# Fifteen short TensorE products and one pair of scores moved in the opening of a fused attention and feed-forward kernel

## The chip, the cores and the metric

The kernel runs on one core of a Trainium2 chip. The metric is the device time of one execution in microseconds (us); less is better. Engines are named as in the profile: PE is TensorE's matmul, PEld its weight load, DVE is VectorE, ACT is ScalarE, POOL is GpSimd, SP is SyncE.

## What is computed

Softmax attention for 8 batches and 12 heads (448 positions, head width 64), then a feed-forward layer with a leaky ReLU on the 3584 x 768 result:

```python
scores = (1 / sqrt(64)) * q @ k.transpose(0, 1, 3, 2)
attn = softmax(scores, axis=-1)
x = (attn @ v).transpose(0, 2, 1, 3).reshape(3584, 768)
h = x @ w_in                       # 768 -> 2048
out = maximum(0.01 * h, h) @ w_out # 2048 -> 768
```

## The kernel before

**Units.** The attention is cut into 48 units of two heads of one batch. Six units (HP) make up one batch's rows. A unit goes through the same steps: load q, k, v by DMA; cast them to bf16 (`cast`, L183; L190 for q and k, L198 for v); turn q and k with eight TensorE transposes and one copy out of PSUM (`transposes`, L294; products at L301, copy at L305); four pairs of score products (`scores`, L311, products at L319, one pair for each quarter of 112 keys); four exponentials on ScalarE (`expo`, L326; the first three write tile `e` at L331, the fourth writes tile `c` at L334); two weighted sums, one for each head (`pv`, L366, sixteen small products at L362 in `pairs`), each followed on VectorE by a reciprocal (L374) and a product (L375) into tile `x`; last, four transposes of `x` (`x_transposes`, L379, L389 and copy at L390).

**Order.** The instruction order of each engine is written out by hand in program order. `first(u)` (L870) issues the first six units as a software pipeline: the scores and exponentials of unit u, the transposes of unit u + 1, the weighted sums of unit u - 1, the x transposes of unit u - 2. After these six, the feed-forward products fill TensorE, and a hand-made model decides where the attention steps of later batches go among them.

**PSUM.** Two banks `g0` and `g1` rotate through `next_bank()` (L74); they hold the transposes and the weighted sums. Three slots `sc0` to `sc2`, of two banks each, rotate through `next_slot()` (L69) and hold the scores; a slot is free when the exponential that reads it has ended. `next_bank()` reverses the list and returns `banks[1]`, so `banks[0]` is the one handed out before the latest.

**Products on zeros.** `warm_up` (L239) issues 128x512 products and `stay_warm` (L243) 128x128 products on a tile of zeros (`warm`, part of `h_mix`, so `hmix` in the profile). Their results are never read. In the kernel before, seven long ones come at the start, one and five short ones behind the two halves of unit 0's transposes (L303), and one long one between unit 0's third and fourth scores (L878).

**What happens in the first units.** In `first(0)` unit 1's transposes follow unit 0's fourth scores on TensorE, then come the casts of unit 2 and of unit 0's v on VectorE (L894, L895). In `first(1)` three scores of unit 1 are followed by unit 2's transposes, unit 0's first weighted sum (`pv(0, 0)`), unit 1's fourth scores (L899) and, at the end, unit 0's second weighted sum (`pv(0, 1)`).

Of the kernel before, what the change touches and what calls it, by code (L numbers as in the profile page):

```python
# [16 lines left out]
def kernel(  # L17
# [9 lines left out]
    nc = tc.nc  # L27
# [3 lines left out]
    P = 128  # L31
# [34 lines left out]
    banks = [ps_g.tile([P, 4 * P], F32, name=f"g{i}") for i in range(2)]  # L66
    slots = [ps_s.tile([P, 2, 512], F32, name=f"sc{i}") for i in range(3)]

    def next_slot():  # L69

        slots.append(slots.pop(0))
        return slots[-1]

    def next_bank():  # L74

        banks.reverse()
        return banks[1]
# [105 lines left out]
    def cast(u, parts=(0, 1, 2), by=nc.gpsimd.tensor_copy):  # L183
        if u >= NU:
            return
        for x in parts:
            f = raw[u].pop(x)
            t = qkb[u % NB]
            if x < 2 and (x == 0 or u < HY):
                by(t[:SC, x].rearrange("p so h d -> p h so d"), f)  # L190
            elif x == 1:
                if u < HY + NB:
                    nc.gpsimd.memset(t[:, 1, KC], 0.0)
                by(t[:, 1, :KC].rearrange("p so h d -> p h so d"), f[:, :, :KC])
                by(t[:D, 1, KC, 0], f[:D, 0, KC])
                by(t[D:, 1, KC, 1], f[:D, 1, KC])
            elif u < HY:
                by(v_old[:, u % NV, :, :, :D], f)  # L198
            else:
                t = v_sb[u % NV]  # L200
                by(t[:, :2 * KC, :D].rearrange("p (h so) d -> p h so d", h=2), f[:, :, :KC])  # L201
                by(t[:D, 2 * KC, :D], f[:D, 0, KC])
                by(t[D:, 2 * KC + 1, :D], f[:D, 1, KC])
# [27 lines left out]
    warm = h_mix.rearrange("p m c t -> p (m c t)")[:, :512]  # L231
# [7 lines left out]
    def warm_up(n):  # L239
        for _ in range(n):  # L240
            nc.tensor.matmul(next_bank(), warm[:, :P], warm, start=True, stop=True)

    def stay_warm(n):  # L243

        ps = next_slot()
        for _ in range(n):
            nc.tensor.matmul(ps[:, 0, :P], warm[:, :P], warm[:, :P], start=True, stop=True)

    warm_up(7)
    nc.vector.memset(qkT_all.rearrange("p u i c s -> p u (i c s)")[:, :, 2 * S:2 * S + EP], 0.0)  # L250
# [39 lines left out]
    def turn_tile(bank):  # L290
        bank = next_bank() if bank is None else bank
        return bank.bitcast(BF16)

    def transposes(u, bank=None):  # L294
        n = SC if u < HY else P
        t, flat = qkb[u % NB], qkT[u % NQ].rearrange("p i c s -> p (i c s)")[:, :2 * NSC * n]
        for parts in ((1,), (0,)) if u == 0 else ((0, 1),):
            tr = turn_tile(bank)[:, :2 * NSC * n].rearrange("p (i s) -> p i s", i=2)
            for i in parts:
                for so in range(NSC):  # L300
                    nc.tensor.transpose(tr[:, i, ts(so, n)], t[:n, i, so].rearrange("p h d -> p (h d)"), ident[:n, :n])  # L301
            if u == 0:
                stay_warm(1 if parts == (1,) else 5)  # L303
            at = slice(parts[0], parts[-1] + 1)
            (nc.scalar.copy if u == 0 and parts == (1,) else nc.vector.tensor_copy)(  # L305
                flat.rearrange("p (i s) -> p i s", i=2)[:, at], tr[:, at]
            )
# [3 lines left out]
    def scores(u, c):  # L311
        ps = next_slot()
        t = qkT[u % NQ]
        sc_t[u, c] = ps
        if u < HY:
            t = t.rearrange("p i c s -> p (i c s)")
            for j in range(2):
                p = slice(j * D, (j + 1) * D)
                nc.tensor.matmul(ps[:, j, :S], t[p, S + c * SC:S + c * SC + P], t[p, :S], start=True, stop=True)  # L319
            return  # L320
        for p, j in ((slice(0, D), 0), (slice(D, P), 1)) if c < KC else ((slice(0, P), 0),):
            nc.tensor.matmul(  # L322
                ps[:, j, :S].rearrange("p (so s) -> p so s", so=NSC), t[p, 1, c], t[p, 0, :, :SC], start=True, stop=True,
            )

    def expo(u, c):  # L326
        e, ps = e_sb[u % NE], sc_t.pop((u, c))
        n = SC if u < HY else P
        if c < KC:
            e = e[:n, :EM].rearrange("p (j c s) -> p j c s", j=2, c=KC)  # L330
            nc.scalar.activation(e[:, :, c, :], ps[:n, :, :S], AX.Exp, scale=scale)  # L331
        elif u < HY:
            e = e_old[u % NE][:n, :2 * S].rearrange("p (j s) -> p j s", j=2)
            nc.scalar.activation(e, ps[:n, :, :S], AX.Exp, scale=scale)  # L334
        else:
            nc.scalar.activation(e[:, EM:EL], ps[:, 0, :S], AX.Exp, scale=scale)
# [29 lines left out]
    def pv(u, j, bank=None):  # L366

        bank = next_bank() if bank is None else bank
        ps = bank[:, :NSC * (D + 1)].rearrange("p (q d) -> p q d", q=NSC)
        pairs(u, j, ps)  # L370
        if j == 0:
            x_t[u] = x_pool.tile([SC, NSC, 2, D], BF16, name="x")
        rec = r_pool.tile([SC, NSC, 1], F32, name="rec")
        nc.vector.reciprocal(rec, ps[:SC, :, D:])  # L374
        nc.vector.tensor_mul(  # L375
            x_t[u][:, :, j, :], ps[:SC, :, :D], rec.to_broadcast([SC, NSC, D])
        )

    def x_transposes(u, bank=None):  # L379
        b, hp = divmod(u, HP)  # L380
        at = place_of(b * S)
        if bank is None:
            x = x_t.pop(u).rearrange("p so h d -> p so (h d)")
            turn(xT_flat[:, hp * NX + at:hp * NX + at + S], x.rearrange("p so n -> p (so n)"))
            return
        dst = xT[:, hp, at:at + S]
        tr = turn_tile(bank)
        for so in range(NSC):
            nc.tensor.transpose(tr[:, ts(so, SC)], x_t[u][:, so], ident[:SC, :SC])  # L389
        nc.vector.tensor_copy(dst, tr[:, :S])  # L390
# [467 lines left out]
    def supply(u):  # L858

        for what, n, *parts in {0: [('load', 6, (0, 1)), ('qk', 3), ('v', 1), ('v', 2), ('load', 6, (2,))], 1: [('qk', 4), ('v', 3), ('load', 8, (0, 1))], 2: [('qk', 5), ('v', 4), ('w', 1)], 3: [('qk', 6), ('v', 5), ('w', 1)], 4: [('qk', 7), ('v', 6), ('load', 10, (0, 1)), ('load', 8, (2,))], 5: [('qk', 8), ('v', 7), ('load', 10, (2,)), ('load', 12)]}[u]:  # L860
            if what == "qk":
                cast(n, (0, 1))
            elif what == "v":
                cast(n, (2,))
            elif what == "load":
                load(n, *parts)
            else:
                load_w(n)

    def first(u):  # L870

        scores(u, 0)
        scores(u, 1)
        if u < 2:
            scores(u, 2)
        expo(u, 0)
        if u == 0:
            warm_up(1)  # L878
        expo(u, 1)
        if u >= 2:  # L880
            x_transposes(u - 2, next_bank())
        if u == 1:
            transposes(u + 1)
        if u >= 1:
            pv(u - 1, 0)
        if u > 1:
            scores(u, 2)
            scores(u, 3)
        if u == 0:
            scores(u, 3)  # L890
        if u != 1:
            transposes(u + 1)
        if u == 0:
            cast(2, (0, 1), fast)  # L894
            cast(0, (2,), fast)  # L895
        if u + 1 < HP:
            supply(u)
        if u == 1:
            scores(u, 3)  # L899
        expo(u, 2)  # L900
        expo(u, 3)
        if u + 1 == HP:
            supply(u)
        if u >= 1:
            pv(u - 1, 1)
# [4 lines left out]
    for u in range(HP):  # L910
        first(u)
# [343 lines left out]
```

## Time and profile before

| | |
|---|---|
| median of 3 runs | 376.85 us |
| the three runs | 376.82, 376.85, 377.42 us |
| profiled execution: its own time | 376.9 us |
| profiled execution: span | 375.1 us |
| PE busy | 368.5 us (98% of the span) |
| DVE, ACT, POOL busy | 255.4, 259.9, 191.8 us |
| granted TensorE clock | 1.00 in the mean |

A line of the timeline has the start in us, the length in us, the engine, the line of the kernel, the operation, the tiles written and read, and the count of merged instructions. In square brackets stands the engine's idle time before it and what ended that. A line of the groups has the busy time in us and the mean of one in ns, then the idle time before such instructions. A line of the chain is one piece of the work that ended last: start, length, and what it was. Matmuls overlap: two or more merged in one line take less than the sum of their lengths, and the end of a matmul is modelled.

### The profile page before, as it was taken

The page shows a single profiled execution, that of the slowest core. Times are in us where ns is not written, and L with a number is a line of the kernel's source. Part 1 is how long each engine was busy: PE and PEld are TensorE (multiplying, and loading weights), DVE is VectorE, ACT ScalarE, POOL GpSimd, SP SyncE. Part 2 cuts the span into 40 slices and gives each one's busy share as a digit, 9 for nine tenths or more (in the row PEclk, how much of TensorE's full clock was granted, in tenths as well). Part 3 has the DMA queues.
Part 4 walks back from the last instruction along what each step waited for, and adds up shares of the span by engine and source line. Part 5 has one row for each costly group of instructions (what it writes and reads, how often), then busy time and mean ns, then how long its engine had stood idle before and what let it go on. Part 6 is the DMA issues. An engine that isn't in the chain of part 4 may idle for free.

```text
span 375.1 us, 10120 instructions
## 1 busy us (share of the span) xinstructions
PE 368.5 (98%) x4004; PEld 265.4 (71%) x4004; DVE 255.4 (68%) x560; ACT 259.9 (69%) x399; POOL 191.8 (51%) x376
## 2 busy tenths in 40 slices
PE   7899999999999999999999999999999999999996
PEld 3665658755698566995569966699665995679865
DVE  4664798767666967676576665875747775685864
ACT  6998795866768785758766587666787658626721
POOL 8976781987269979634488335692347020000000
PEclk9999999999999999999999999999999999999999
DMA  9999999999499967973979648989447640221123
GB/s 156 198 203 206 184 195 203 161 163 177 94 189 151 125 136 92 197 160 52 140 145 147 141 66 75 170 134 192 62 67 103 136 112 0 75 62 40 47 66 105
DMA packets 99920, 48.08 MB, mean 128 GB/s; under 512 B 64672, under 2 KB 96928, under 8 KB 99872
## 3 DMA queue, kind: packets, MB, share of 16 engines
q0 software_dynamic: 39600, 22.47, 45.4%
q1 hardware_dynamic: 60080, 24.84, 34.0%
q8 instruction: 31, 0.51, 0.6%
q14 instruction: 17, 0.14, 0.1%
q10 hardware_dynamic: 192, 0.12, 0.1%
HBM read 45.61 MB, written 11.01 MB: 151 GB/s over the span
## 4 chain that ended last, share of the span: by engine, by line
PE 95%; DMA 2%; DVE 1%; POOL 1%; ACT 0%; issue 0%; POOLq 0%; ACTq 0%
PE g L683 30%; PE g L548 14%; PE sc L548 14%; PE sc L322 7%; PE sc L350 6%; PE g L424 4%; PE sc L319 4%; PE sc L645 4%; PE sc L362 3%; PE g L827 2%; PE sc L343 2%; DMA w_in_mix<-in_v_dram 2%; PE g L362 1%; PE g L301 1%; PE sc L424 1%; POOL w_in_mix L163 1%
## 5 line engine op out<-in xcount | busy, mean ns | idle before, releaser
L331 ACT ACTIVATE e<-sc 128x896 bf16<-128x896 f32 (+1 forms) x144 | 123.6, 923 | 30.0 <-PE sc L322 20.5
L683 PE MATMUL g<-w_out_sb,h 128*128 128x384 bf16 (+1 forms) x440 | 84.1, 325 | 0.0
L683 PEld LDWEIGHTS <-h 128*128 128x128 bf16 x592 | 54.4, 98 | 41.1 <-issue 10.6
L537 ACT ACTIVATE h<-c 128x512 bf16<-128x512 f32 (+1 forms) x72 | 43.1, 610 | 29.9 <-DVE c L563 12.4
L548 PEld LDWEIGHTS <-w_in_sb 128*128 128x128 bf16 x576 | 54.6, 98 | 5.7
L190 POOL COPY qkb<-fq 112x512 bf16<-112x512 bf16 x34 | 23.2, 683 | 44.4 <-DMA qkT<-qkb 35.2
L548 PEld LDWEIGHTS <-w_in_mix 128*128 128x128 bf16 x432 | 40.6, 98 | 3.7
L201 POOL COPY v<-fv 128x384 bf16<-128x384 bf16 x30 | 18.8, 627 | 41.8 <-PE sc L350 39.2
L688 DVE COPY o<-g 128x384 f32<-128x384 f32 x47 | 26.0, 554 | 14.4 <-PE g L683 14.2
L983 DVE RECIPROCAL rec<-sc 112x8 f32<-112x8 f32 x42 | 8.7, 207 | 38.0 <-PE sc L350 21.6
L350 PE MATMUL sc<-v,e 128*128 128x65 bf16 x720 | 33.3, 193 | 0.0
L322 PE MATMUL sc<-qkT 64*128 64x448 bf16 (+1 forms) x210 | 32.8, 352 | 0.0
L350 PEld LDWEIGHTS <-e 128*128 128x128 bf16 x720 | 31.2, 98 | 1.3
L984 DVE TENSOR_TENSOR x<-sc,rec 112x512 bf16<-112x512 f32 x42 | 29.0, 691 | 1.5
L548 PE MATMUL g<-xT,w_in_sb 128*128 128x256 bf16 (+1 forms) x216 | 28.5, 268 | 0.0
L548 PE MATMUL sc<-xT,w_in_sb 128*128 128x256 bf16 (+1 forms) x216 | 28.5, 268 | 0.0
L694 DVE TENSOR_TENSOR o<-o,g 128x384 f32<-128x384 f32 x39 | 21.4, 550 | 8.9 <-PE g L683 4.2
L343 PE MATMUL sc<-v,e 128*128 128x130 bf16 x120 | 26.5, 221 | 0.0
L649 DVE TENSOR_TENSOR o<-o,sc 128x192 f32<-128x192 f32 x39 | 13.7, 351 | 18.3 <-PE sc L645 18.3
L683 PE MATMUL g<-w_mix,h 128*128 128x384 bf16 x128 | 24.6, 326 | 0.0
L163 POOL DMA_DIRECT2D fv<-in_v_dram x32 | 20.1, 640 | 7.4 <-DMA fq<-in_q_dram 3.1
L683 PE MATMUL g<-w_mix,hmix 128*128 128x384 bf16 x112 | 21.7, 326 | 0.0
(149 smaller groups left out, 741.2 us busy)
## 6 DMA issues: line engine op xcount, KB each, us to landing
fq<-in_q_dram POOLq DMA_DIRECT2D x17, 224.0 KB, 6.2
w_out_sb<-in_moe_w_out_dram POOLq DMA_DIRECT2D x4, 768.0 KB, 13.1
out_dram<-o SPq DMA_DIRECT2D x7, 336.0 KB, 3.5
w_in_sb<-in_moe_w_in_dram POOLq DMA_DIRECT2D x2, 1152.0 KB, 13.2
out_dram<-o SPq DMA_DIRECT2D x7, 288.0 KB, 3.6
fk<-in_k_dram POOLq DMA_DIRECT2D x15, 128.0 KB, 6.2
fv<-in_v_dram POOLq DMA_DIRECT2D x15, 128.0 KB, 5.2
fk<-in_k_dram POOLq DMA_DIRECT2D x15, 96.0 KB, 6.3
```

Source lines behind the costliest of these rows:

```text
L163: nc.gpsimd.dma_start(out=t[p, :n, :, :so].rearrange("p u h so d -> p (u h) (so d)"), in_=(q, k, v)[x][b, hs, keys].rearrange("h (p so) d ...
L190: by(t[:SC, x].rearrange("p so h d -> p h so d"), f)
L322: nc.tensor.matmul(ps[:, j, :S].rearrange("p (so s) -> p so s", so=NSC), t[p, 1, c], t[p, 0, :, :SC], start=True, stop=True,)
L331: nc.scalar.activation(e[:, :, c, :], ps[:n, :, :S], AX.Exp, scale=scale)
L343: nc.tensor.matmul(ps, e[:, EM + qc * SC:EM + qc * SC + P], vt[:, 2 * KC:].rearrange("p j d -> p (j d)"), start=True, stop=False, skip_gro ...
L350: nc.tensor.matmul(ps[:, j * (D + 1):(j + 1) * (D + 1)], e[:, at:at + P], vt[:, j * KC + c], start=False, stop=(c == KC - 1), skip_group_c ...
L537: nc.scalar.activation(hs[:, m:m + 2, cols], x.rearrange("p (m t) -> p m t", m=2), AX.Prelu, alpha=0.01)
L548: nc.tensor.matmul(ps[:, j * nh:(j + 1) * nh], w[:, kk, ts(j, P)], x[:, kk], start=(first and j == 0 and kk == 0), stop=(kk == KH - 1), sk ...
L683: nc.tensor.matmul(ps[:, cols], x[:, m], w[:, m], start=(first and m == 0), stop=(m == MH - 1), skip_group_check=True,)
L688: by(o[:, at], ps[:, :NW])
L694: nc.vector.tensor_add(o[:, at], o[:, at], ps[:, :NW])
L984: nc.vector.tensor_mul(x, ps[:, :, :, :D], rec.to_broadcast([SC, 2, 2 * NP, D]))
```

## The change

`stay_warm` can be given a PSUM bank; without one it takes a slot, as before. In `first(0)` four short products stand between unit 0's fourth scores and unit 1's transposes, and eight behind those transposes. In `first(1)` unit 1's fourth scores come directly behind unit 2's transposes, followed by three short products, and only then unit 0's two weighted sums. The order of the exponentials on ScalarE, and the orders of VectorE, GpSimd and SyncE, are as before. The rotation of banks and slots is as before too.

```diff
-    def stay_warm(n):
+    def stay_warm(n, ps=None):
 
-        ps = next_slot()
+        ps = next_slot()[:, 0, :P] if ps is None else ps[:, :P]
         for _ in range(n):
-            nc.tensor.matmul(ps[:, 0, :P], warm[:, :P], warm[:, :P], start=True, stop=True)
+            nc.tensor.matmul(ps, warm[:, :P], warm[:, :P], start=True, stop=True)
...
         if u == 1:
             transposes(u + 1)
+            scores(u, 3)
+            stay_warm(3, banks[0])
         if u >= 1:
             pv(u - 1, 0)
         if u > 1:
...
             scores(u, 3)
         if u == 0:
             scores(u, 3)
+            stay_warm(4, banks[0])
         if u != 1:
             transposes(u + 1)
         if u == 0:
+            stay_warm(8, banks[0])
             cast(2, (0, 1), fast)
             cast(0, (2,), fast)
         if u + 1 < HP:
             supply(u)
-        if u == 1:
-            scores(u, 3)
         expo(u, 2)
```

## The prediction

> **What bounds the kernel now.** I read the page first (busy shares, then the chain that ended last), then the groups of TensorE instructions after 20 us, then the pieces of the chain in order of time, and last the timeline of 4 to 16 us, engine by engine.
>
> ```profile
> PE 368.5 (98%) x4004; PEld 265.4 (71%) x4004; DVE 255.4 (68%) x560; ACT 259.9 (69%) x399; POOL 191.8 (51%) x376
> ...
> PE 95%; DMA 2%; DVE 1%; POOL 1%; ACT 0%; issue 0%; POOLq 0%; ACTq 0%
> ```
> ```profile
> L319 PE MATMUL sc<-qkT 64*128 64x448 bf16 x108 | 14.0, 353 | 0.2 <-ACT e L331 0.2
> ```
>
> The first two lines are of the page, the third is one of the groups of TensorE in 20 to 376 us, where it is the only one with idle time before it: 0.2 us. So after the opening TensorE is never short of work, and this change, whose edits all lie before 12 us, can move the end only by moving the moment at which the dense stretch begins. The chain shows what sets that moment:
>
> ```profile
> 3.70 6.39 DMA w_in_mix<-in_v_dram
> ...
> 10.60 0.67 PE g L362 x16
> 11.27 0.30 PE sc L319 x2
> 11.57 0.63 PE g L362 x16
> ...
> 15.51 0.55 PE sc L319 x4
> 16.06 0.37 PE g L389 x4
> 16.43 0.51 PE g L362 x16
> ...
> 20.77 0.97 ACT e L331
> ...
> 21.77 0.55 PE sc L319 x4
> ```
>
> Unit 0's values land at about 10.1 us, VectorE casts them, and from 10.60 us the chain is one weighted sum (L362), unit 1's fourth scores (L319, the piece at 11.27 that the change moves), and the other weighted sum. The chain touches ScalarE last at 20.77 us; from 21.77 us TensorE is the bound for good.
>
> ScalarE runs beside it almost without a break. Single exponentials, from the timeline of ScalarE in short windows:
>
> ```profile
> 8.70 0.93 ACT L334 ACTIVATE c<-sc 112x896 bf16<-112x896 f32 x1
> ...
> 9.50 0.94 ACT L331 ACTIVATE e<-sc 112x896 bf16<-112x896 f32 x1
> ...
> 11.89 0.97 ACT L334 ACTIVATE c<-sc 112x896 bf16<-112x896 f32 x1
> ...
> 15.07 1.01 ACT L334 ACTIVATE c<-sc 112x896 bf16<-112x896 f32 x1
> ...
> 15.97 0.92 ACT L331 ACTIVATE e<-sc 112x896 bf16<-112x896 f32 x1
> ```
>
> They start 0.80 us apart (8.70 to 9.50, and three in 2.39 from 9.50 to 11.89), except once: 0.90 from 15.07 to 15.97, where unit 3's first scores came late. ScalarE thus has 0.10 us to win in this stretch and no more: at 15.87 us it would itself be the limit.
>
> **The price of one short product.** A 128-column product on zeros stands in the trace only with the clock still low; products with the clock up stand beside it:
>
> ```profile
> 4.53 0.31 PE L247 MATMUL sc<-hmix 128*128 128x128 bf16 x1
> ...
> 5.01 0.74 PE L247 MATMUL sc<-hmix 128*128 128x128 bf16 x5
> ...
> 7.55 0.41 PEld L301 LDWEIGHTS <-qkb 112*128 112x128 bf16 x8 [0.20 <-DVE qkb L190]
> ```
> ```profile
> L319 PE MATMUL sc<-qkT x36: 346/359/549, 5.7 to 18.8; 64*128 64x448 bf16 x36
> ```
>
> One such product takes 0.31 us from start to end, so five in 0.74 are (0.74 - 0.31)/4 = 0.107 apart. The eight weight loads at 7.55, each ahead of a transpose of 112 columns, come at most 0.41/8 = 0.05 apart. The last row (the scores in 0 to 20 us) says when the rate changed: the longest, 549 ns, is in the first ones at 5.7 us, the median is 359. All fifteen new products come after 7.4 us, where the neighbours run at the high rate: I take 0.05 each, with 0.107 as the upper end. They do no work that anything else was to do, so below zero there is nothing.
>
> **Edit 1, four products before unit 1's transposes.**
>
> ```profile
> 7.26 0.36 PE L319 MATMUL sc<-qkT 64*128 64x448 bf16 x2 [0.23 <-ACT e L331]
> ...
> 7.56 0.57 PE L301 MATMUL g<-ident,qkb 112*128 112x112 bf16 x8
> ...
> 8.16 0.62 DVE L305 COPY qkT<-g 128x896 bf16<-128x896 bf16 x1 [0.72 <-PE g L301]
> ...
> 8.85 0.55 PE L319 MATMUL sc<-qkT 64*128 64x448 bf16 x4 [0.72 <-ACT e L331]
> ...
> 9.47 0.29 DVE L190 COPY qkb<-w_in_mix 112x512 bf16<-112x512 bf16 x1 [0.48 <-DMA w_in_mix<-in_k_dram]
> ```
>
> The score pair at 7.26 occupies the array until about 7.45 (four scores in 0.55, two in 0.36: 0.19 a pair). The transposes wait for VectorE's cast until 7.55. Four products end at 7.45 + 4 x 0.05 = 7.65, so the transposes, the copy behind them and unit 1's first scores go about 0.1 later: 8.85 becomes 8.95, done 9.31. ScalarE takes these scores at 9.50, when it is through with its earlier exponentials: 0.29 us of cover (8.85 + 0.36 = 9.21), of which 0.19 stays. On the path: 0. With the cover gone it would cost 0.10, at the low rate 0.43. On VectorE the casts of unit 2 stand behind the copy; the second waits for its load until 9.47 anyway, so nothing passes on.
>
> **Edit 2, eight products after them.** They start at about 8.07 and take 8 x 0.05 = 0.40, to 8.5; the scores behind them wait for VectorE's copy until 8.95. Hidden, with 0.45 to spare; at the low rate they take 0.86 and just fit. They write the bank that nobody reads at that time. On the path: 0.
>
> **Edit 3, unit 1's fourth scores before the weighted sums, with three products between.**
>
> ```profile
> 9.68 0.36 PE L319 MATMUL sc<-qkT 64*128 64x448 bf16 x2 [0.28 <-ACT c L334]
> ...
> 9.98 0.57 PE L301 MATMUL g<-ident,qkb 112*128 112x112 bf16 x8
> ...
> 10.66 0.62 DVE L305 COPY qkT<-g 128x896 bf16<-128x896 bf16 x1
> ...
> 11.21 0.36 PE L319 MATMUL sc<-qkT 64*128 64x448 bf16 x2
> ...
> 11.50 0.27 PE L362 MATMUL g<-x_mix,e 112*128 112x65 bf16 x3
> ...
> 12.22 0.18 DVE L374 RECIPROCAL rec<-g 112x4 f32<-112x4 f32 x1 [0.27 <-PE g L362]
> ...
> 12.44 0.42 DVE L375 TENSOR_TENSOR x<-g,rec 112x256 bf16<-112x256 f32 x1
> ...
> 12.92 0.37 PE L389 MATMUL g<-ident,x 112*128 112x112 bf16 x4 [0.25 <-DVE x L375]
> ```
>
> In its new place the score pair waits for the PSUM slot that unit 1's first exponential frees: 9.50 + 0.94 = 10.44, and with 0.05 from such a release to the start (8.70 + 0.93 = 9.63 to 9.68), 10.49. This is an added wait; the first weighted sum stands behind it on TensorE, its reciprocal and product on VectorE behind that. The pair takes 0.19 (to 10.68), three products 0.15 (to 10.83). The first sum starts at about 10.85 in place of 10.60, takes 0.51 (the piece at 16.43, with nothing between), and the second follows at once, at 11.36 to 11.38 in place of 11.50; its bank is free when the copy at 10.66 ends, 11.28. So the second sum is 0.12 to 0.14 earlier. VectorE's work on the first sum, later by 0.25, now lies just ahead of that on the second: if the product there holds VectorE for its full 0.42, the reciprocal of 12.22 comes at about 12.2, if the next instruction overlaps its end, at 12.1. I take 12.12. **Gain 0.10 us.** Its ends: 0.16 (11.50 less the free bank, with 0.06 to the start), of which ScalarE below lets through 0.10; if the switch from the added products to the sum costs the 0.10 that the switch from scores to sum costs now (11.21 + 0.19 = 11.40 to 11.50), or VectorE is held, about 0.02; with products at 0.107, a loss of about 0.05. The exponential of the moved scores cannot start sooner than 11.89, since ScalarE is full. The orders of ScalarE, VectorE, GpSimd and SyncE stay; no DMA is moved.
>
> **What is late next.** Unit 0's transposes go from 12.92 to 12.82, and in TensorE's order unit 1's first sum, unit 2's later scores and unit 3's transposes follow 0.10 earlier; the scores of 15.51 are then at 15.41 and the exponential of 15.97 at 15.87, where ScalarE has no more to give. From there both engines run 0.10 earlier, through 20.77, and the dense stretch starts at 21.67, not 21.77. The sum: 0 + 0 - 0.10. The profiled execution took 376.9 us for a span of 375.1, and the median of the runs is 376.85, so the profile stands for the median: **376.8 us**. A measurement of this kernel can tell about 0.2%, 0.75 us, from no change; the forecast is well within it.
>
> **The clock.** The rows show one change of rate, about 6 us, and no return: eight transposes take 0.57 at 7.56 and 0.57 at 9.98, though TensorE idled 0.72 and 0.28 us between. The Trainium skill, "TensorE: Matmul & The Clock Gate", section "What's actually happening", says that the clock falls back after at least one idle window of about 3.4 us; by that rule the products guard against nothing here, and the trace agrees.
>
> **Rivals.**
> *Nothing arrives* (376.9): the switch to the first sum, or VectorE's back-to-back work, eats the gain. For it: the 0.10 from 11.40 to 11.50. Against: the sums at 16.43 and elsewhere run without a gap in themselves.
>
> *Slower, the clock comes late.* If the rate rises only after 7.45 us, the transposes at the low rate use up the cover of 0.29 by themselves, and the four products, 4 x 0.107 = 0.43, delay unit 1's first exponential and all of ScalarE behind it by 0.43. The moved scores wait for that exponential and the sums for them; if the low rate lasts past 11 us, the pair's further 0.19, the three products' 0.32 and 0.05 of ends come on top: +0.43 to +1.0, 377.3 to 377.9. It decides from a rise at 7.45 us on. Against: the profile has the rise 1.4 us sooner. For: one of the three times is 377.42, 0.6 over the others. The same section of the Trainium skill's page holds the moment to vary between runs, since the window runs free; no row here shows a second moment.
>
> *Faster, the old kernel falls back to the low clock in some executions.* From 10.60 the chain has 0.67 + 0.30 + 0.63 + 0.37 = 2.0 us of TensorE on rows above, which would be doubled; the new products would prevent it, up to 2 us, 374.8. Against: all shown times lie within 0.6 us. The Trainium skill's section "Part 4: PE-mode transpose" of that page says that transposes do not count as activity in the same way, which speaks for it: the stretch without other work would be 7.62 to 8.85. The trace shows no fall behind it.
>
> **How the numbers follow.** The gain of 0.1: 0.48. Nothing arrives: 0.27. Late clock: 0.15, of which 0.10 beyond 377.6. Fall-back in the old kernel: 0.10, all beyond 0.2%. So faster 0.10, same 0.80, slower 0.10. The range: below, the forecast less 0.5, as far as the shown runs differ with no cause known (376.3); above, the late clock's lower price and the slowest run shown (377.4).
>
> **What would show it right or wrong.** Right: fifteen more products at L247, 0.05 apart; unit 1's first exponential still at 9.50; the first sum near 10.85, the second near 11.37; no 0.10 lost on ScalarE before its exponential of 15.97; the dense stretch 0.1 sooner. Wrong: that first exponential after 9.50, the second sum after 11.50, the new products 0.107 apart, or a time below 376.1 or above 377.6.

## The result, and the profile after

The changed kernel takes 377.78 us in the median of 16 runs (377.39 to 378.38); the kernel before takes 377.01 in 16 runs (376.49 to 377.48). The ratio is 1.0022, with a 95% interval of 1.0014 to 1.0030: slower by about 0.8 us. The profiled execution took 377.84 us for a span of 376.1. The forecast was 376.8, with 377.4 as the upper end.

**The opening went nearly as drawn.** From the timeline of the changed kernel, 7 to 16 us (start, length, engine, line, operation):

```profile
7.47 0.40 PE L247 MATMUL g<-hmix 128*128 128x128 bf16 x4
7.70 0.56 PE L301 MATMUL g<-ident,qkb 112*128 112x112 bf16 x8
8.10 0.61 PE L247 MATMUL g<-hmix 128*128 128x128 bf16 x8
...
10.40 0.36 PE L319 MATMUL sc<-qkT 64*128 64x448 bf16 x2
...
10.70 0.34 PE L247 MATMUL g<-hmix 128*128 128x128 bf16 x3
10.88 0.26 PE L362 MATMUL g<-x_mix,e 112*128 112x65 bf16 x3
...
11.39 0.26 PE L362 MATMUL g<-x_mix,e 112*128 112x65 bf16 x3
...
12.15 0.17 DVE L374 RECIPROCAL rec<-g 112x4 f32<-112x4 f32 x1
```
```profile
6.20 0.92 ACT L331 ACTIVATE e<-sc 112x896 bf16<-112x896 f32 x1 [0.90 <-PE sc L319]
...
9.41 0.94 ACT L331 ACTIVATE e<-sc 112x896 bf16<-112x896 f32 x1
...
14.99 1.01 ACT L334 ACTIVATE c<-sc 112x896 bf16<-112x896 f32 x1
...
15.88 0.93 ACT L331 ACTIVATE e<-sc 112x896 bf16<-112x896 f32 x1
```

Eight products take 0.61 and three 0.34, so one adds about 0.054; the first weighted sum starts at 10.88 (10.85 drawn) and the second at 11.39 (11.37 drawn). But the gap before the exponential of unit 3 is 0.89 us (14.99 to 15.88), where 0.80 was expected. The whole of ScalarE is 0.09 sooner in this execution from its first exponential on, before any edit; in the kernel before that one starts at 6.29:

```profile
6.29 1.72 ACT L331 ACTIVATE e<-sc 112x896 bf16<-112x896 f32 x2 [0.99 <-PE sc L319]
```

Unit 0's first six scores take 0.85 us here and 1.01 there, and this exponential waits for the first of them. So nothing of a gain reaches ScalarE: from its first exponential to that of unit 3 it is 9.68 us in both kernels (6.29 to 15.97, 6.20 to 15.88). The switch from scores to products cost 0.11 (10.40 + 0.19 = 10.59, to 10.70); the sum follows the products with almost no gap (10.70 + 3 x 0.054 = 10.86, to 10.88).

**The loss comes 45 to 60 us later.** The dense stretch starts 0.09 sooner (21.68, not 21.77), and then TensorE, which in the kernel before waited 0.2 us in all after 20 us, waits more. Groups of TensorE in 20 to 376 us, and the timeline near 56 and 60 us, of the changed kernel:

```profile
L389 PE MATMUL sc<-ident,x 112*128 112x112 bf16 x12 | 1.1, 214 | 0.5 <-DVE x L986 0.5
```
```profile
56.52 0.56 DVE L436 TENSOR_TENSOR w_mix<-w_out_sb 128x768 bf16<-128x768 bf16 x1 [0.99 <-DMA w_out_sb<-in_moe_w_out_dram]
...
59.64 0.37 PE L389 MATMUL sc<-ident,x 112*128 112x112 bf16 x4 [0.33 <-DVE x L986]
...
61.31 0.37 PE L389 MATMUL sc<-ident,x 112*128 112x112 bf16 x4 [0.16 <-DVE x L986]
```
```profile
  DMA qkT<-qkb: 0.5, 1
```

The last row is of the waits of L319 between 70 and 76 us. In the kernel before, the row at L436 reads:

```profile
55.73 0.56 DVE L436 TENSOR_TENSOR w_mix<-w_out_sb 128x768 bf16<-128x768 bf16 x1 [0.33 <-DMA w_out_sb<-in_moe_w_out_dram]
```

A load of `w_out` lands 0.79 us later. VectorE stands at L436 for it; the reciprocal and product of a unit stand behind L436, TensorE's transposes of x behind these, in the order of each engine. Twelve microseconds on, scores wait for a DMA transpose of q and k. It is issued at 67.40, 0.32 later than in the kernel before, and lands at 73.30, 1.77 later. Its time from issue to landing (L276, the first issue after 66 us), before and after:

```profile
DMA to landing us min/median/max: 4.5/4.5/4.5
DMA to landing us min/median/max: 5.9/5.9/5.9
```

Set instruction against instruction, by the times of the kernel before, TensorE is 0.07 ahead at 50 us, 0.53 behind at 59.1, 0.79 at 60.5 and 0.97 at 72.4, and keeps that to the end. The last of these waits sets the total: the scores start at 73.34, directly behind the landing, so what TensorE lost at 59 to 61 us only makes the wait at 73 us shorter.

**What the DMA queues did.** The page's queue rows hardly differ (these are of the changed kernel; the kernel before has 17 in the second):

```profile
q8 instruction: 31, 0.51, 0.6%
q14 instruction: 18, 0.14, 0.1%
```

The row q8 is the fetch of TensorE's own instructions: 31 packets, 0.51 MB, 16 KB each. Stretch by stretch the difference appears. The first row below is 54 to 56 us of the kernel before, the second the same of the changed kernel (the engines' busy time, then clock, DMA share and GB/s):

```profile
54.00:56.00 2.00, 2.00 (x20) 1.07 (x19) 1.64 (x4) 1.59 (x4) 0.46 (x2) 1.00 1.18 202
```
```profile
54.00:56.00 2.00, 2.00 (x20) 1.07 (x18) 1.50 (x4) 1.60 (x4) 1.10 (x2) 1.00 1.20 124
```

202 GB/s against 124, with the DMA engines just as busy: 78 GB/s less over 2 us is 0.77 us of the full rate. In the trace's packet records twenty data packets of that stretch take 0.6 to 1.1 us instead of about 0.13, all begun between 54.28 and 54.78, and a fetch of TensorE's instructions begins at 53.62. In the kernel before, that fetch begins at 56.08, with no such packets. By its place in the stream it is the same fetch: about 1290 TensorE instructions have been recorded when it begins, in both kernels. The changed kernel has 30 instructions more before that point (15 products and 15 weight loads), so it gets there 30 instructions of work sooner.

### The profile page after: what moved, and what is told of

It is laid out like the page before. It is cut to its first block, busy times and chain, and to the rows that moved or that the text cites. A ratio compares the mean times of both kernels' runs of the same rounds, so it can differ in the third digit from the quotient of the medians.

```text
span 376.1 us, 10150 instructions
## 1 busy us (share of the span) xinstructions
PE 369.6 (98%) x4019; PEld 266.3 (71%) x4019; DVE 256.7 (68%) x560; ACT 260.1 (69%) x399; POOL 192.1 (51%) x376
## 3 DMA queue, kind: packets, MB, share of 16 engines
q0 software_dynamic: 39600, 22.47, 44.6%
## 4 chain that ended last, share of the span: by engine, by line
PE 96%; DVE 1%; ACT 1%; issue 0%; DVEq 0%; ACTq 0%
PE g L683 30%; PE sc L548 14%; PE g L548 14%; PE sc L322 7%; PE sc L350 6%; PE sc L319 4%; PE g L424 4%; PE sc L645 4%; PE sc L362 3%; PE g L827 2%; PE sc L343 2%; PE g L301 1%; PE g L362 1%; ACT e L331 1%; PE g L241 1%; PE sc L424 1%
## 5 line engine op out<-in xcount | busy, mean ns | idle before, releaser
L201 POOL COPY v<-fv 128x384 bf16<-128x384 bf16 x30 | 17.8, 593 | 44.3 <-PE sc L350 41.1
```

## The experiments

**First theory (A).** The first reading blamed a collision at 43.7 us: with VectorE 0.07 earlier and GpSimd 0.08 later, GpSimd's copy took 0.99 us and not 0.62, and the loads of `w_out` behind it issued 0.46 later. The rivals were that the products themselves cost (B), and that the late landing was chance (C).

*e1, the move without the products* (the three added `stay_warm` lines taken out of the change):

```diff
-            stay_warm(3, banks[0])
...
-            stay_warm(4, banks[0])
...
-            stay_warm(8, banks[0])
```


> The fourth scores of the second unit moved as in the change, none of the fifteen products. Theory A (the opening is a gain, and the loss comes later: VectorE then runs a little earlier against GpSimd near 43.7 us, GpSimd's copy there takes 0.99 instead of 0.62 us, the loads of w_out issue about 0.46 us later and land about 0.8 later, VectorE waits for them at L436 and TensorE behind it): the dense stretch starts 0.1 us sooner than in the kernel before, the copy collides, w_out lands late, time about 377.8 (+0.8). Theory B (the fifteen products themselves cost the time): as the kernel before, 377.0, or 0.1 less. Theory C (the lateness of w_out is a chance of the one profiled execution, and the loss has another place): no fixed relation; the profile tells where.

Median 376.99, ratio 1.0005 (0.9992 to 1.0019). The move is worth nothing that can be measured, and A's +0.8 is not there.

*e2, the products without the move* (the change with `scores(u, 3)` put back behind `supply(u)`):

> The fifteen products where the change has them, the fourth scores left in their old place. Theory A: the opening gains nothing, so the race at 43.7 us goes as before and the time is that of the kernel before, 377.0 (within 0.2). Theory B: +0.8, 377.8. Theory C: no fixed relation.

Median 377.73 (377.01 to 378.20), 0.7 above the 377.01 of the kernel before on that chip. The ratio, 1.0011 (0.9994 to 1.0028), doesn't separate them, since eight of that chip's 35 runs of the kernel before lie at 378.2 to 381.4, outside the bulk of 376.5 to 377.4; so medians and the bulk are given from here on. The products carry the loss, not the move. That speaks for B against A.

*e3, VectorE nudged in the changed kernel, and e4, GpSimd nudged in the kernel before:*

```diff
+                if m == 8:
+                    for _ in range(4):
+                        nc.vector.memset(gate[:, 1:], 0.0)
                 for _ in range({5: 3, 7: 2, 8: 1, 9: 1, 10: 1, 12: 2, 13: 2}.get(m, 0)):
```


> The changed kernel with four VectorE memsets of one column (about 0.06 us each) ahead of the VectorE operation that begins at 43.69 us, so that GpSimd's copy of 43.72 us begins first, as in the kernel before. Theory A: that copy takes 0.62 again, w_out issues 0.4 us earlier, and most of the loss is gone: 376.9 to 377.2. Theories B and C: the loss stays, 377.8.


```diff
+        if g == 10:
+            for _ in range(3):
+                nc.gpsimd.memset(word, 0.0)
         if r < 3:
```


> The kernel before with three GpSimd memsets of two columns (about 0.1 us each) ahead of the copies that precede the three loads of w_out at 44.20 us, so that GpSimd's second copy begins after VectorE's operation of 43.76 us. Theory A: that copy takes 0.99, the loads issue 0.5 to 0.7 us later, w_out lands late and the time is that of the changed kernel or a little above, 377.7 to 378.1. Theories B and C: no change, 377.0.

e3 did what it was to do; GpSimd's rows at 43 us (a copy in each of the first two, then the loads of `w_out`):

```profile
42.50 0.62 POOL L190 COPY qkb<-w_mix 112x512 bf16<-112x512 bf16 x1
43.05 0.62 POOL L190 COPY qkb<-o 112x512 bf16<-112x512 bf16 x1
43.60 1.48 POOL L215 DMA_DIRECT2D w_out_sb<-in_moe_w_out_dram  x2
```

The copy takes 0.62 again, the loads issue a microsecond sooner than in the changed kernel, and the second load lands at 55.65, only 0.11 later than in the kernel before. Yet TensorE waits at the same two places, loses 0.18 us near 60 and 0.48 near 72, and the time is 377.56, ratio 1.0019 (1.0009 to 1.0030). Theory A falls, and with it the late `w_out` as the main cost. e4 made no collision (in that execution VectorE was later too, and the copy took 0.61), so its 377.32, ratio 0.9998 (0.9971 to 1.0025), tells nothing on A.

**Second theory (F).** The traces of the first six kernels had a pattern: in the three with 30 more TensorE instructions the fetch comes at 53.6 to 54.1 us and slow packets follow; in the three without, it comes at 56.1 to 56.6 and none do. So not what the products are or where they stand would cost, but how many instructions they are.

*e5, the same count with no product in a new place:*

```diff
-    warm_up(7)
+    warm_up(2)
+    for _ in range(5):
+        ps = next_bank()
+        for x in range(4):
+            nc.tensor.matmul(ps[:, ts(x, P)], warm[:, :P], warm[:, ts(x, P)], start=True, stop=True)
```


> The kernel before, with five of its seven long products on zeros at the start cut into four of 128 columns each: the same time on TensorE (4 x 0.107 = 0.43 us, one long one is 0.43 us there), but 30 TensorE instructions more, as many as the change adds, and none of them in a new place. Theory F (the fifteen products cost by their number: every later fetch of TensorE's instructions, 16 KB on the instruction queue, comes 30 instructions sooner in the work; the fetch of 56.1 us comes at about 53.6, while w_out and a DMA transpose are in flight; all queues then stand for 0.8 us, w_out lands later, VectorE waits at L436 and TensorE behind it): slower as the change is, 377.5 to 377.9, with the fetch at 53.5 to 54.5 us and slow packets behind it. Theory B (the products cost where they stand, in 7.4 to 11 us): 377.0, as the kernel before.

Fetch at 53.76, sixteen slow packets from 54.52, and this stretch:

```profile
54.00:56.00 2.00, 2.00 (x21) 1.03 (x19) 1.46 (x3) 1.60 (x3) 0.00 (x0) 1.00 1.21 140
```

Median 377.62; its 12 runs lie between 377.14 and 377.90, the bulk of the kernel before (29 of 35 runs) between 376.59 and 377.45. The ratio, 1.0005 (0.9990 to 1.0020), shows no difference; the six runs of the kernel before at 378.4 to 379.7 pull it. But every run of e5 lies above the kernel before's median of 377.03. TensorE waits at 60.8 and 73.2 us, as in the changed kernel. Theory F called it; B did not, and C's chance is out as well: the loss comes back with the count.

*e6, the change with 8 instructions instead of 30, and e10, with 2.* In e6 one product of 512 columns replaces the four, two of 512 the eight, one of 384 the three. e10 also cuts the five short ones behind unit 0's transposes as one of 512 and one of 128. e9 is the changed kernel itself on the chip of e10.

```diff
-            stay_warm(3, banks[0])
+            stay_warm_long((3 * P,), banks[0])
...
-            stay_warm(4, banks[0])
+            stay_warm_long((4 * P,), banks[0])
...
-            stay_warm(8, banks[0])
+            stay_warm_long((4 * P, 4 * P), banks[0])
```


> The changed kernel with its products on zeros cut otherwise: one of 512 columns for the four, two of 512 for the eight, one of 384 for the three. TensorE is filled for the same time at the same places, with 8 instructions more than the kernel before instead of 30. Theory F: the fetch comes at about 55.4 us, when the second load of w_out has nearly landed, and most of the loss is gone: 376.9 to 377.3. Theory B: the loss stays, 377.7.

> The changed kernel itself once more, to stand on the same chip as the next one. Theory F: 377.5 to 378.0, fetch of TensorE's instructions at 53.5 to 54.2 us, slow packets behind it.

> The changed kernel with its products on zeros cut long (four products of up to 512 columns for the fifteen) and, further, one of 512 and one of 128 columns for the five of 128 behind unit 0's transposes: TensorE is filled for the same time at the same places, and the number of its instructions is that of the kernel before plus 2. Theory F: the fetch stays at about 56 us, no slow packets at 54 to 55.5, time 376.8 to 377.1, that is the kernel before or 0.1 less. Theory B (the products cost where they stand): 377.7.

e6 has its fetch at 55.84, no slow packets behind it and no wait of TensorE after 21.6 us; its profiled execution took 376.86, but its 12 runs scatter from 376.54 to 379.58 with median 377.49, above the 376.9 to 377.3 that theory F gave. The ratio is 1.0010 (0.9987 to 1.0034), which holds both no loss and the whole of it, so e6 is inconclusive. e9 and e10 speak more clearly. On one chip the kernel before has a median of 376.92, the changed kernel 377.71, ratio 1.0029 (1.0018 to 1.0039), and e10, with TensorE filled for the same time at the same places, 376.95, ratio 1.0010 (0.9986 to 1.0033; one run at 381.31). Nine of e10's eleven runs lie below 377.48, where the changed kernel's eight begin. The stretch of e10:

```profile
54.00:56.00 2.00, 2.00 (x20) 1.05 (x19) 1.90 (x5) 1.59 (x4) 0.55 (x1) 1.00 1.17 201
```

*e7 and e8, VectorE's work on `w_out` moved behind the attention steps,* in the changed kernel and in the kernel before:

```diff
-                for _ in range({14: 3}.get(m, 0)):
-                    next(outs)
...
-            for _ in range((3, 4, 2, 2, 1, 0, 0, 0)[x]):
+            for _ in range((4, 4, 3, 2, 2, 0, 0, 0)[x]):
```


> The changed kernel with the three VectorE operations on w_out that stand at 56.5 us (L436, L438, L436) moved behind unit 10's and 11's copies, to about 60 us and later. Theory F: w_out still lands late, but nothing of the attention stands behind the wait any more: 376.9 to 377.1. Theory B: the loss stays, 377.7.

> The kernel before with the same three operations moved. Theory F: the kernel before hardly waits there (0.33 us at L436, none of it on TensorE), so within 0.2 of 377.0. Theory B: the same.

e7 missed: 377.73, ratio 1.0008 (0.9992 to 1.0024). The wait at 60 us is gone, but at 73.85 us the scores wait 1.1 us, as the groups of TensorE have it:

```profile
L319 PE MATMUL sc<-qkT 64*128 64x448 bf16 x108 | 14.2, 354 | 1.3 <-DVE h L702 1.1 <-ACT e L331 0.2
```

The row names VectorE; the waits of L319 in that stretch name the DMA transpose of q and k with 1.6 us. It is issued at 67.48 and lands at 73.80. So the wait near 60 us was not what the change costs: with it gone, TensorE waits the longer for the transpose. e8 is 377.00, ratio 0.9991 (0.9972 to 1.0011), as expected.

*e11, 42 instructions more,* all seven long products cut in four:

> The kernel before with all seven long products at the start cut into four each: 42 TensorE instructions more, the same time on TensorE. Theory F: the fetch moves to 52 to 53.5 us, still while w_out's second load and a DMA transpose are in flight; slow packets behind it, 377.4 to 377.9. Theory B: 377.0. If only a shift of exactly 30 matters, 377.0 too.

Fetch at 53.60 (52 to 53.5 expected), twenty slow packets from 54.05, and scores that wait 0.4 us at 73.1. The median is 377.20, about a third of the loss and less than expected; the ratio, 1.0004 (0.9988 to 1.0019), doesn't tell it from none. In its profiled execution (377.59) TensorE was 0.15 to 0.20 later than in the kernel before by then, and the late `w_out` cost it nothing. Why its other runs lose less than those of e5 isn't settled.

*e12, no DMA transpose in flight:*

```diff
-            owed_x.append((u, model["now"] + {X_PE[0]: 4.0, X_PE[1]: 2.5, X_PE[2]: 2.4}[u]))
+            owed_x.append((u, model["now"] + {X_PE[0]: 3.0, X_PE[1]: 4.0, X_PE[2]: 2.5, X_PE[3]: 2.4}[u]))
...
-    X_PE = (HP + 3, HP + 4, HP + 5)
+    X_PE = (HP + 2, HP + 3, HP + 4, HP + 5)
```


> The changed kernel with unit 8's x transposed on TensorE rather than by a DMA transpose, so that no DMA transpose is in flight at 54 us; otherwise as the change, with 30 TensorE instructions more than before and 8 for the transposes. One look. Theory F with the transpose as its condition: a fetch at 53 to 54 us with no slow packets behind it, and w_out's second load landing by 55.5 us. If the fetch alone stalls the queues: slow packets as in the changed kernel.

```profile
54.00:56.00 2.00, 2.00 (x14) 0.73 (x13) 1.93 (x5) 1.50 (x3) 0.70 (x1) 1.00 1.15 210
```

A fetch at 54.20 and no slow packet, the full 210 GB/s, `w_out`'s second load in at 54.14. (The time, 385.25, is not of interest: the new place of the transposes upsets the planned order, and TensorE loses 8 us near 60.) So in this one trace a fetch without a DMA transpose in flight has no slow packets behind it. That the second load was already in is not the reason: in e2 it was in before the fetch too (53.79, fetch at 54.13), and seventeen slow packets follow.

All fourteen traces side by side, worked out from the packet, landing and instruction records: start of the fetch; data packets over 0.6 us in 53 to 57 us; landing of the second load of `w_out`; landing of the first transpose of q and k issued after 65 us; what TensorE lost against the kernel before from 50 to 62 us, and from 71 to 80 us; median:

```
                 instr.  fetch us  slow packets  w_out[1] us  qkT us  by 62  at 72  median us
before             0      56.08        0           55.54       71.53    -      -     377.01
after            +30      53.62       20           56.33       73.30   0.85   0.19   377.78
e1 move only       0      56.62        0           55.76       71.72  -0.08   0.00   376.99
e2 products only +30      54.13       17           53.79       71.03  -0.09   0.00   377.73
e3 DVE nudge     +30      53.6        18           55.65       72.91   0.18   0.48   377.56
e4 POOL nudge      0      56.5         0           55.30       71.10  -0.09   0.00   377.32
e5 warm-up split +30      53.76       16           55.85       73.12   0.19   0.49   377.62
e6 coarse         +8      55.84        0           55.38       71.41   0.08   0.06   377.49
e7 outs, after   +30      53.94       20           56.11       73.80  -0.09   1.30   377.73
e8 outs, before    0      55.88        0           55.19       70.98  -0.09   0.00   377.00
e9 after again   +30      53.56       21           55.86       73.10   0.42   0.48   377.71
e10 zero          +2      56.02        0           55.16       70.96  -0.08   0.00   376.95
e11 split 7      +42      53.60       20           55.63       73.04  -0.09   0.58   377.20
e12 no DMA turn  +38      54.20        0           54.14       70.08    -      -     385.25
```

Seven of seven with a fetch by 54.2 us and a DMA transpose in flight have the slow packets; none of the other seven has. The median is of all of a kernel's runs and the rest of one profiled execution, so a row can differ: e2's execution, at 377.01, is the fastest of its twelve.

**The transpose of q and k sets the loss.** In the six traces in which it lands at 72.9 us or later, the scores that need it start 0.04 to 0.05 us behind its landing, and TensorE is from there on behind the kernel before by that landing less 72.32 us: 0.98, 0.59, 0.80, 1.49, 0.79 and 0.72. In the other seven executions that keep the order of the kernel before, it lands by 71.72 and nothing waits for it; e2's is one of them, which is how it escaped. What the late `w_out` cost TensorE before is swallowed by this later wait in all six.

Two things make the transpose late. One is the later issue: 0.32 us in the changed kernel, but e9 and e11 issue it sooner than the kernel before (66.91 and 66.84 against 67.08) and it is late all the same. The larger is its time from issue to landing, 5.8 to 6.3 us in the six, 4.5 to 4.8 in the seven. Of the 1.45 us more in the changed kernel, 0.56 pass before its first packet (1.85 us after the issue, against 1.29), the rest while it moves. In the six the next fetch of TensorE's instructions (70.8 to 71.5 us) begins 2.1 to 2.3 us before the landing, and 0.43 to 0.48 us behind it come 16 to 19 slow packets; in the seven it begins between 0.3 us before the landing and 0.5 after it, and 2 to 11 follow within 1.5 us. So the pattern of theory F is there twice. That this second fetch is the cause is not shown: no run moves it alone.

## Why the prediction was wrong, point by point

- **Edits 1 and 2: 0 on the path.** Right. They were hidden: ScalarE took unit 1's first scores at 9.41, 0.80 behind its earlier exponential, with no break, and each product cost about 0.054.
- **Edit 3: gain 0.10.** The pair starts at 10.40, the 10.49 drawn less this execution's 0.09. Then the switch from scores to products cost 0.11, which stands at nothing in the sum. The prediction named a switch of 0.10 as a lower end of its gain, but from the products to the sum, where almost none is seen. Less the 0.09, both sums came 0.11 to 0.12 later than drawn; that 10.88 and 11.39 look like 10.85 and 11.37 is luck, as is the dense stretch that starts 0.09 sooner. The order gained nothing that reaches ScalarE, and e1 shows no gain that can be measured.
- **"No DMA is moved."** This is the step that failed. No data transfer is, but 30 TensorE instructions are also 1.9 KB (0.51 MB over some 8,000 of them, 64 bytes each) of a stream that the same DMA engines fetch in blocks of 16 KB. Each later fetch moved against the work: the one at 56.08 us came at 53.62. In the sum this term stood at nothing; it is worth +0.8 us. e5 (the count without the products' places, median 0.6 up) and e10 (the places without the count, median as before) show the count as the cause from both sides; the way from the fetch to the late transpose is read from the traces alone.
- **"TensorE is never short of work, so this change can move the end only by moving the moment at which the dense stretch begins."** The 0.2 us of idle time was true and the inference was not: it says nothing of how close the transfers run behind. In the kernel before, the transpose of q and k landed at 71.53, 0.84 us before the scores that need it (72.37); in the changed one it landed 1.77 later, and TensorE waited.
- **The rivals.** The late clock was no part of it: products and transposes run at the high rate in both kernels. A second moment of the rise, which the prediction had no row for, may be seen here: the longest of the first scores takes 549 ns in the kernel before and 462 in the changed one, which would be a sooner rise and not a later one. The fall-back of the clock isn't in any trace looked at. The "slower" side had the right sign by another mechanism. "Nothing arrives" was right for the opening.

The Trainium skill, "Runtime: NRT & Kernel Launch", section "Instruction fetch mechanics", has the sequencer fetch the next 16 KiB block, 256 instructions, over its own DMA queue while it runs the current one, at a cost that is mostly hidden. The trace agrees on the block (31 packets of 16,384 bytes, 0.51 MB), and TensorE shows no wait for a fetch: after 20 us it waits 0.2 us in all in the kernel before, for ScalarE. The cost shows on the other queues, which near 54 us moved 0.77 us' worth less.

## What to carry to other kernels

Instructions that do no work still make up the instruction stream: before filling gaps with many short products, fill them with few long ones, and after any change in their number look where the instruction fetches fall among the tight transfers. A bound engine with no idle time doesn't mean that nothing else is near the path: read the waits of the engines next to it for the transfers that land just in time. And when a small change far from the loss is slower, compare the two traces instruction by instruction, and follow them from the first place where they part to the last wait: an earlier wait can be swallowed by a later one, as e7 shows.

## What the runs showed of the hardware

A fetch of TensorE's instructions that starts near 54 us, while a DMA transpose shares the queues with large loads, was followed in seven traces of seven by 16 to 21 packets of 0.6 to 1.4 us each instead of about 0.13 (100 to 155 GB/s from 54 to 56 us, against 201 to 212 in the six kernels that fetch near 56). The fetch near 62 us, with no DMA transpose in flight, has no slow packets in any of the fourteen traces, and neither has e12's at 54.20. A fetch near 56 us, at the very end of the third transpose, was harmless in six kernels, so a transpose in flight is not the whole condition.

Nor is a fetch needed: between 68.1 and 70.6 us, with transposes of q and k in flight, every trace has 10 to 18 slow packets, and no fetch of TensorE's begins between 63.3 and 70.7. From 43.2 to 44.6 us, with a transpose in flight, every trace has 2 to 24, in five of them begun before the fetch there. What stops the queues, and why there, stays open: no run moves one fetch alone.
